# Sums over tokens as one full-array product per batch, gate values as four products with block-diagonal weights, both casts of a bank pair ahead of both subtractions, and four joint places

## The chip, the cores and the metric

The kernel runs on one core of one Trainium2 chip. The metric is the device time of one execution in microseconds, the median of the runs of a kernel. A core has a matrix engine (TensorE, PE in the rows; its weight loads stand apart as PEld), a vector engine (VectorE, DVE), a scalar engine (ScalarE, ACT), GpSimd (POOL) and a sync engine (SyncE, SP), which issues nearly all transfers here. TensorE can be used as one array of 128x128 or as several tiles; a row such as `64*32` gives the tile's rows and columns.

## The reference, cut to what matters

Eight batches, eight heads, 576 tokens, 64 channels a head, 32 memory slots; then a mixture of eight experts over 4608 tokens of 512 channels, hidden width 1024.

```python
a = np.exp(phi - np.max(phi, axis=2, keepdims=True))
a = a / (np.sum(a, axis=2, keepdims=True) + 1e-09)      # over tokens
k_m = np.einsum('bhsm,bhsd->bhmd', a, k)
v_m = np.einsum('bhsm,bhsd->bhmd', a, v)
scores = scale * np.matmul(q, k_m.transpose(0, 1, 3, 2))
attn = softmax(scores)
x = rows(np.matmul(attn, v_m))
...
logits = x @ w_gate + modality_bias[modality_id]
e_idx = np.argmax(logits, axis=1)
gate_w = softmax(logits)[np.arange(N), e_idx]
...
h = np.maximum(x[mask] @ w1[e], 0.0)
out[mask] = gate_w[mask, None] * (h @ w2[e])
```

## The kernel before, in words

**Tiling.** Batches go in pairs, two half-arrays of 64 rows (`NG` = 2 groups `g`) by four strips of 32 columns (`HG` = 4 heads a group). The memory products `kv_products` (L408) use TensorE as eight tiles of 64x32: 72 matmuls over nine chunks of tokens, written `64*32` in the rows. Each float32 matmul of this kind leaves two records in the trace, so 72 are x144 there. The sums of the exponentials over the tokens (`sums`, folded over the chunks by GpSimd long before) follow in the same tiles: eight matmuls of one column against `ones_c` (L416). They give the softmax's denominators `den`, `rec` on VectorE, with which ScalarE scales the products into `kvn`. `first_products` and `first_sums` are the forms for batch 0.

**Weights folded into values.** The expert's first weights are multiplied by the memory values once per batch: `value_products` (L776, 64*32, eight matmuls for each half of 512 hidden columns), then split into a high part `vwh` (a cast by ScalarE) and a low part `vwl` (the product less the cast, by VectorE). The attention weights `xa`, `xb` are split into high and low likewise (`xah`, `xal`, `xbh`, `xbl`). `hidden` (L831) and `outputs` (L868) then run three full-array products for each tile, high by high, low by high, high by low. These two lines are nearly all of the matrix work. `relu` gives `hh` (ScalarE, L844) and `hl` (VectorE, L848), `gated` gives `ob` (ScalarE, L881), which is stored by SP.

**Gate.** `mem_gate` (L546) multiplies the memory values by `w_gate` in eight matmuls 64*32 of eight columns, at the end of the scores (L571) of the same batch; `gate_values` (L554) copies the two groups' results from two banks to `vg` with two VectorE copies. `logits` (L713) reads `vg` later, as 128*32 tiles.

**Order.** Nothing is left to a scheduler. A planner, `weave`, merges a list of attention stages with a list of expert stages by estimated takes (`TAKES`) and due times, and the calls are issued in that order on every engine. The table `JOINT` says, for batch b, behind which output step (tile, f) the joint stands; tile `None` counts as 4, and a batch without an entry has (2 + b % 2, 7). A joint is: the kv products of batch b+2, the sums, the value products of batch b+1 for the first half of the columns (into two single banks of `pe`) and for the second half (`other_values`, into a pair of banks), and the two transposes (`turn`, L150) of `kvn`. The functions themselves call the casts and subtractions, so ScalarE and VectorE have these queued in the order of the calls. There are four single PSUM banks `pe`, used in turn, and two pairs.

**The split of a pair.** `value_split` goes bank by bank, cast then subtraction (`split`). In a pair both banks are one PSUM tile, and the program makes the second bank's cast on ScalarE wait for the first bank's subtraction on VectorE; for the single banks there is no such wait.

## Time and profile before

| | |
|---|---|
| median of 3 runs | 381.92 us (380.41 to 382.25) |
| profiled execution | 380.38 us, span 378.6 us |
| mean granted clock of TensorE | 0.998 |
| TensorE busy | 370.4 us, 98% of the span |
| VectorE, ScalarE, GpSimd busy | 66%, 37%, 12% |
| TensorE's share of the chain that ended last | 88% |

Of the profile one reads first who is busy, then the chain of waits, then the timeline of TensorE at the places that the change touches. The start times of successive matmuls tell what one costs; its busy time is longer, since matmuls overlap in the array, and the times on the rows of a group are of its first instruction.

### The profile page before, as it was taken

How to read it: one execution, taken by the hardware profiler on the slowest of the kernel's cores; microseconds unless marked ns; L12 is line 12 of the kernel's file. 1: busy time of each engine (PE TensorE's matmuls, PEld its weight loads, DVE VectorE, ACT ScalarE, POOL GpSimd, SP SyncE). 2: the span in 40 equal slices, each digit the busy share in tenths (PEclk: the TensorE clock that was granted, in tenths of full speed). 3: DMA queues.
4: the chain of work that ended last, by engine and by line, in shares of the span. 5: the costliest groups of instructions: out<-in, count | busy, mean ns of one | idle time of the engine just before them, and what ended most of it. 6: DMA issues, size and time to landing. Idle time of an engine off the chain costs nothing.

```text
span 378.6 us, 9983 instructions
## 1 busy us (share of the span) xinstructions
PE 370.4 (98%) x4045; PEld 308.5 (81%) x4045; DVE 248.6 (66%) x618; ACT 139.7 (37%) x328; POOL 46.1 (12%) x110
## 2 busy tenths in 40 slices
PE   6899999999999999999999999999999999999996
PEld 2677887889878898898987889797987979697986
DVE  4788758885958797868855689567874538750400
ACT  2382433524344054323415244431623306240401
POOL 3148030022130030004000030004000000000000
PEclk9999999999999999999999999999999999999999
DMA  8999668969969547583653737760232102321112
GB/s 290 348 377 239 110 121 250 292 114 304 282 113 287 216 72 141 155 311 61 110 167 99 270 70 128 214 205 2 56 110 74 29 2 55 119 64 30 30 35 56
DMA packets 93979, 56.89 MB, mean 150 GB/s; under 512 B 69732, under 2 KB 75108, under 8 KB 93924
## 3 DMA queue, kind: packets, MB, share of 16 engines
q1 hardware_dynamic: 93648, 55.87, 53.9%
q8 instruction: 33, 0.54, 0.6%
q10 hardware_dynamic: 276, 0.30, 0.2%
q14 instruction: 22, 0.18, 0.2%
HBM read 37.28 MB, written 18.87 MB: 148 GB/s over the span
## 4 chain that ended last, share of the span: by engine, by line
PE 88%; DVE 5%; DMA 3%; ACT 2%; issue 1%; SPq 1%; ACTq 0%; DVEq 0%
PE pe L868 48%; PE pe L831 26%; PE pair L408 4%; DMA raw<-in_moe_w_dram 2%; PE pe L776 2%; PE pair L571 2%; PE pe L912 2%; PE pair L776 1%; PE pair L713 1%; DMA ph<-in_phi_dram 1%; DVE vwl L156 1%; PE pair L150 1%; DVE top L310 1%; DVE a L650 0%; DVE sa L640 0%
## 5 line engine op out<-in xcount | busy, mean ns | idle before, releaser
L868 PE MATMUL pe<-w2h,hh 128*128 128x512 f32 x280 | 111.3, 397 | 0.0
L868 PE MATMUL pe<-w2h,hl 128*128 128x512 f32 x280 | 109.4, 391 | 0.0
L868 PE MATMUL pe<-w2l,hh 128*128 128x512 f32 x280 | 107.2, 391 | 0.0
L848 DVE SCALAR_TENSOR_TENSOR hl<-pe,hh 128x256 fp32r<-128x256 f32 (+2 forms) x158 | 56.7, 389 | 35.3 <-ACT hh L844 34.6
L844 ACT ACTIVATE hh<-pe 128x256 fp32r<-128x256 f32 (+2 forms) x158 | 52.5, 361 | 33.2 <-PE pe L831 32.6
L868 PEld LDWEIGHTS pe<-w2h,hh 128*128 128x128 f32 x280 | 52.6, 188 | 11.9 <-DVE vwl L156 0.8
L868 PEld LDWEIGHTS pe<-w2l,hh 128*128 128x128 f32 x280 | 52.5, 188 | 11.2
L868 PEld LDWEIGHTS pe<-w2h,hl 128*128 128x128 f32 x280 | 52.7, 188 | 9.8
L881 ACT ACTIVATE ob<-pe,gates 128x512 f32<-128x512 f32 x35 | 23.9, 688 | 68.6 <-PE pe L868 40.2
L831 PE MATMUL pe<-xbh,vwh 128*128 128x320 f32 x128 | 40.3, 314 | 0.1
L831 PE MATMUL pe<-xbh,vwl 128*128 128x320 f32 x128 | 39.6, 309 | 0.0
L831 PE MATMUL pe<-xbl,vwh 128*128 128x320 f32 x128 | 39.6, 309 | 0.0
L831 PE MATMUL pe<-xah,vwh 128*128 128x256 f32 x124 | 35.3, 287 | 0.4 <-DVE hl L848 0.4
L831 PE MATMUL pe<-xal,vwh 128*128 128x256 f32 x124 | 34.9, 283 | 0.0
L831 PE MATMUL pe<-xah,vwl 128*128 128x256 f32 x124 | 34.9, 283 | 0.0
L831 PEld LDWEIGHTS pe<-xah,vwh 128*128 128x128 f32 x124 | 23.6, 192 | 2.7 <-ACT vwl L793 0.8
L831 PEld LDWEIGHTS pe<-xbh,vwh 128*128 128x128 f32 x128 | 24.0, 188 | 1.4 <-issue 0.5
L344 POOL COPY ts<-tm 32x4 f32<-32x4 f32 x24 | 5.0, 210 | 165.2 <-DVE tm L336 164.4
L831 PEld LDWEIGHTS pe<-xbl,vwh 128*128 128x128 f32 x128 | 24.1, 188 | 0.3
L831 PEld LDWEIGHTS pe<-xbh,vwl 128*128 128x128 f32 x128 | 24.0, 188 | 0.0
L831 PEld LDWEIGHTS pe<-xal,vwh 128*128 128x128 f32 x124 | 23.7, 192 | 0.2
L831 PEld LDWEIGHTS pe<-xah,vwl 128*128 128x128 f32 x124 | 23.7, 192 | 0.0
(178 smaller groups left out, 465.5 us busy)
## 6 DMA issues: line engine op xcount, KB each, us to landing
out_dram<-ob SPq DMA_DIRECT2D x72, 128.0 KB, 2.4
q_sb<-in_q_dram SPq DMA_DIRECT2D x112, 72.0 KB, 3.1
kv_sb<-in_k_dram SPq DMA_DIRECT2D x6, 1152.0 KB, 6.4
kv_sb<-in_v_dram SPq DMA_DIRECT2D x6, 1152.0 KB, 9.2
ph<-in_phi_dram SPq DMA_DIRECT2D x13, 288.0 KB, 8.1
kv_sb<-in_k_dram SPq DMA_DIRECT2D x4, 576.0 KB, 5.6
kv_sb<-in_v_dram SPq DMA_DIRECT2D x4, 576.0 KB, 6.1
raw<-in_moe_w_dram SPq DMA_DIRECT2D x2, 1024.0 KB, 7.8
```

Of the source, the lines that this page charges most:

```text
L150: nc.tensor.transpose(dst, src, ident[:rows, :rows])
L156: nc.vector.tensor_tensor(l, src, h.bitcast(F32), op=ALU.subtract)
L344: nc.gpsimd.tensor_copy(ts_[BL * a:BL * (a + 1)], live["tm"][BL * o:BL * (o + 1)])
L408: nc.tensor.matmul(live["kvp"][M * j:M * (j + 1), g], lhsT=pe[half, j, c * M:(c + 1) * M], rhs=kv_sb[half, :, j, c * D:(c + 1) * D], start ...
L571: nc.tensor.matmul(sc[g][M * j:M * (j + 1), a, 0:QC * BL], lhsT=kvT[b][rows, 0, M * j:M * (j + 1)], rhs=qT[rows, j, a], start=True, stop=T ...
L776: nc.tensor.matmul(pvs[g][M * j:M * (j + 1), :], lhsT=vT[b][rows, j, :], rhs=raw1[rows, j, cols], start=True, stop=not more, tile_position ...
L831: nc.tensor.matmul(ph[:, 0:n], lhsT=(vl if k == 2 else vh)[:, g, cols], rhs=xl if k == 1 else xh, start=(g == k == 0), stop=(g == NG - 1 a ...
L844: nc.scalar.activation(hs[0][:, f, h0:h0 + p1 - p0], live["ph", f][:, p0:p1], AF.Relu)
L848: nc.vector.scalar_tensor_tensor(hl, live["ph", f][:, p0:p1], 0.0, hh.bitcast(F32), op0=ALU.max, op1=ALU.subtract)
L868: nc.tensor.matmul(po, lhsT=tile_columns(hl if n == 1 else hh, f, t), rhs=(w2l if n == 2 else w2h)[:, f, :], start=(f == n == 0), stop=(f ...
L881: nc.scalar.activation(ob, po, AF.Copy, scale=gate_of(b, t))
L912: nc.tensor.matmul(po, lhsT=x, rhs=w2s[w][:, f, cols], start=(f == i == 0), stop=(f == FCH - 1 and i == 2),)
```

## The change

It does five things. The eight sum products of a batch become one product of the whole array, `sums` of all heads as weights and an indicator `groups` (128x2, one for the rows of group g, else zero) as the moving side. The eight gate products become four of 128 rows by 32 columns with 16 moving columns, whose weights `wg` hold `w_gate` in two diagonal blocks and zeros elsewhere; so one copy to `vg` is enough instead of two. `wg` is set to zero by GpSimd and loaded by two DMAs on SP instead of one, between the two halves of the first expert weights (`raw`). `value_split` calls both casts, then both subtractions. And in `JOINT` the joint of b=2 goes from (2, 1) to (3, 1), that of b=3 from (3, 6) to (3, 4), that of b=5 from (3, 7) to (4, 6).

```diff
-    JOINT = {1: (4, 1), 2: (2, 1), 3: (3, 6)}
+    JOINT = {1: (4, 1), 2: (3, 1), 3: (3, 4), 5: (4, 6)}
...
+    groups = const.tile([P, NG], F32, name="groups")
...
-    wg = const.tile([P, KCH, E], F32, name="wg")
+    wg = const.tile([P, KCH, NG, E], F32, name="wg")
...
-        nc.sync.dma_start(wg, w_gate.rearrange("(a p) e -> p a e", p=P))
+        for g in range(NG):
+            rows = slice(D * g, D * (g + 1))
+            nc.sync.dma_start(wg[rows, :, g], w_gate.rearrange("(a p) e -> p a e", p=P)[rows])
...
-        for j in range(HG):
-            for g in range(NG):
-                half = slice(QP * g, QP * (g + 1))
-                nc.tensor.matmul(
-                    pk[M * j:M * (j + 1), g, 2 * D:2 * D + 1], lhsT=sums[half, j], rhs=ones_c[half],
-                    start=True, stop=True, tile_position=(QP * g, M * j),
-                )
+        nc.tensor.matmul(live["psum"], lhsT=sums.rearrange("p j m -> p (j m)"), rhs=groups, start=True, stop=True)
...
         for j in range(HG):
-            for g in range(NG):
-                rows = slice(D * g, D * (g + 1))
-                nc.tensor.matmul(
-                    to[g][M * j:M * (j + 1), 0, GATE:GATE + E], lhsT=vT[b][rows, j], rhs=wg[rows, j],
-                    start=True, stop=True, tile_position=(D * g, M * j),
-                )
+            nc.tensor.matmul(
+                to[0][M * j:M * (j + 1), 0, GATE:GATE + NG * E], lhsT=vT[b][:, j], rhs=wg[:, j].rearrange("p g e -> p (g e)"),
+                start=True, stop=True, tile_position=(0, M * j),
+            )
...
-        for g in range(NG):
-            nc.vector.tensor_copy(vg[b // 2][:, g, o:o + E], to[g][:, 0, GATE:GATE + E])
+        nc.vector.tensor_copy(
+            vg[b // 2][:, :, o:o + E], to[0][:, 0, GATE:GATE + NG * E].rearrange("p (g e) -> p g e", g=NG)
+        )
...
     def value_split(hf):
-        for g, pv in enumerate(live.pop(("pv", hf))):
-            split([x[:, g, hf * 512:(hf + 1) * 512] for x in vws], pv)
+        value_upper(hf)
+        value_lower(hf)
...
+        nc.gpsimd.memset(wg, 0.0)
```

In the order of TensorE, the joint of b=5 (kv products of batch 7, value products of batch 6) stood like this before; 24 output steps of tile `None` follow the transposes, and hidden products behind them.

```order
L408 MATMUL pair_3972<-kv_sb,exp 32x128 x72
L416 MATMUL pair_3972<-ones_c,sums 32x1 x8
L776 MATMUL pe<-raw_104,kvT_84 32x512 x8
L776 MATMUL pair_4074<-raw_104,kvT_84 32x512 x8
L150 MATMUL pair_4087<-ident,kvn 128x128 x2
L868 MATMUL pe<-w2h,hh 128x512
L868 MATMUL pe<-w2h,hl 128x512
L868 MATMUL pe<-w2l,hh 128x512
L868 MATMUL pe<-w2h,hh 128x512
```

Now, with the lines of the changed kernel (L411 for L408, L765 for L776, L151 for L150, L857 for L868, L820 for L831):

```order
L411 MATMUL pair_3925<-kv_sb,exp 32x128 x72
L416 MATMUL pair_3925<-groups,sums 128x2
L765 MATMUL pe<-raw_105,kvT_85 32x512 x8
L765 MATMUL pair_4020<-raw_105,kvT_85 32x512 x8
L151 MATMUL pair_4033<-ident,kvn 128x128 x2
L857 MATMUL pe<-w2h,hh 128x512
L857 MATMUL pe<-w2h,hl 128x512
L857 MATMUL pe<-w2l,hh 128x512
L820 MATMUL pe<-xah,vwh 128x256
L820 MATMUL pe<-xal,vwh 128x256
```

The sums are one instruction in another tiling, between products of eight tiles; and the joint moved behind 21 of the 24 output steps, so that three are left ahead of the hidden products of batch 6, which read the new `vwh` and `vwl`.

At the end of the scores of a batch, on TensorE, the gate values stood like this before.

```order
L571 MATMUL pair_2567<-q_sb_99,kvT_82 32x288
L546 MATMUL pair_2566<-wg,kvT_82 32x8
L546 MATMUL pair_2567<-wg,kvT_82 32x8
L546 MATMUL pair_2566<-wg,kvT_82 32x8
L546 MATMUL pair_2567<-wg,kvT_82 32x8
L546 MATMUL pair_2566<-wg,kvT_82 32x8
L546 MATMUL pair_2567<-wg,kvT_82 32x8
L546 MATMUL pair_2566<-wg,kvT_82 32x8
L546 MATMUL pair_2567<-wg,kvT_82 32x8
L868 MATMUL pe<-w2h,hh 128x512
```

Now:

```order
L560 MATMUL pair_2522<-q_sb_100,kvT_83 32x288
L560 MATMUL pair_2523<-q_sb_100,kvT_83 32x288
L534 MATMUL pair_2522<-wg,kvT_83 32x16 x4
L857 MATMUL pe<-w2h,hh 128x512
L857 MATMUL pe<-w2h,hl 128x512
```

Eight instructions in the tiling of the scores became four in a tiling that neither neighbour has.

On ScalarE, the joint of b=1 (value products of batch 2), before; in brackets is the engine whose semaphore an instruction waits for.

```order
L690 CAST xah<-aT 128x512
L155 CAST vwh<-pe 128x512 [waits PE_49] x2
L155 CAST vwh<-pair_1852 128x512 [waits PE_49]
L155 CAST vwh<-pair_1852 128x512 [waits DVE_49]
L528 COPY kvT_81<-pair_1865 128x256 [waits PE_49]
```

Now:

```order
L679 CAST xah<-aT 128x512
L774 CAST vwh<-pe 128x512 [waits PE_49] x2
L774 CAST vwh<-pair_1820 128x512 [waits PE_49]
L774 CAST vwh<-pair_1820 128x512
L518 COPY kvT_82<-pair_1833 128x256 [waits PE_49]
```

The rows stand in the same order; the second cast of the pair has lost its wait for VectorE.

## Rows read from the trace of the kernel before

**Rows 1.** The page's busy times of the engines (busy us, share of the span, instructions) and the shares of the chain that ended last.

```profile
PE 370.4 (98%) x4045; PEld 308.5 (81%) x4045; DVE 248.6 (66%) x618; ACT 139.7 (37%) x328; POOL 46.1 (12%) x110
...
PE 88%; DVE 5%; DMA 3%; ACT 2%; issue 1%; SPq 1%; ACTq 0%; DVEq 0%
```

**Rows 2.** The group of the sums among TensorE's instructions by line, whole span: busy us and mean ns of one, then idle time before them.

```profile
L416 PE MATMUL pair<-ones_c,sums 64*32 64x1 f32 x112 | 2.3, 169 | 0.0
```

**Rows 3.** TensorE in order of time, at a place where output products (128*128) give way to value products (64*32) and come back: start us, busy us, line, operation, names, shapes, count.

```profile
60.43 0.39 PE L868 MATMUL pe<-w2h,hl 128*128 128x512 f32 x1
60.65 0.39 PE L868 MATMUL pe<-w2l,hh 128*128 128x512 f32 x1
60.97 1.09 PE L776 MATMUL pe<-raw,kvT 64*32 64x512 f32 x16
```

**Rows 4.** The same view at the joint of b=2: the sums, the value products, the two transposes.

```profile
147.50 0.26 PE L416 MATMUL pair<-ones_c,sums 64*32 64x1 f32 x13
147.60 0.61 PE L776 MATMUL pe<-raw,kvT 64*32 64x512 f32 x1
...
149.63 0.44 PE L150 MATMUL pair<-ident,kvn 128*128 128x128 f32 x2
149.82 0.48 PE L868 MATMUL pe<-w2h,hh 128*128 128x512 f32 x1
```

**Rows 5.** The same view at the joint of b=1, from the first value product to the transposes.

```profile
110.93 0.59 PE L776 MATMUL pe<-raw,kvT 64*32 64x512 f32 x1
...
112.79 0.44 PE L150 MATMUL pair<-ident,kvn 128*128 128x128 f32 x2
```

**Rows 6.** The same view at the end of a batch's scores: the gate products and the output product behind them.

```profile
172.48 0.25 PE L546 MATMUL pair<-wg,kvT 64*32 64x8 f32 x16
172.66 0.50 PE L868 MATMUL pe<-w2h,hh 128*128 128x512 f32 x1
```

**Rows 7.** The chain of waits between 28 and 46 us (start us, us, what), and ahead of its last row TensorE's last product before 43 us from the timeline.

```profile
31.55 0.17 DVE vg L554
...
32.01 0.17 DVE vg L554
...
42.45 0.70 ACT ob L881
...
42.74 0.31 PE L831 MATMUL pe<-xbh,vwl 128*128 128x320 f32 x1
...
43.19 2.02 PE pe L831 x12
```

**Rows 8.** VectorE in order of time at the joint of b=1; in brackets the idle time before an instruction and what ended it.

```profile
116.39 0.63 DVE L156 TENSOR_TENSOR vwl<-pair,vwh 128x512 fp32r<-128x512 f32 x1
117.66 0.69 DVE L156 TENSOR_TENSOR vwl<-pair,vwh 128x512 fp32r<-128x512 f32 x1 [0.65 <-ACT vwh L155]
118.27 0.81 DVE L650 TENSOR_TENSOR a<-a,ra 128x640 f32<-128x640 f32 x1
...
119.95 0.38 DVE L848 SCALAR_TENSOR_TENSOR hl<-pe,hh 128x256 fp32r<-128x256 f32 x1
121.10 0.76 DVE L848 SCALAR_TENSOR_TENSOR hl<-pe,hh 128x256 fp32r<-128x256 f32 x2 [0.77 <-ACT hh L844]
```

**Rows 9.** ScalarE in the same stretch.

```profile
117.05 0.59 ACT L155 CAST vwh<-pair 128x512 fp32r<-128x512 f32 x1 [2.78 <-DVE vwl L156]
...
120.06 0.72 ACT L690 CAST xbh<-aT 128x640 fp32r<-128x640 f32 x1 [1.29 <-DVE aT L656]
120.69 1.20 ACT L844 ACTIVATE hh<-pe 128x256 fp32r<-128x256 f32 x4
```

**Rows 10.** TensorE in the same stretch, hidden products of batch 2.

```profile
119.82 0.28 PE L831 MATMUL pe<-xal,vwh 128*128 128x256 f32 x1
119.94 0.28 PE L831 MATMUL pe<-xah,vwl 128*128 128x256 f32 x1
120.39 0.39 PE L831 MATMUL pe<-xah,vwh 128*128 128x256 f32 x1 [0.17 <-DVE hl L848]
...
121.08 0.28 PE L831 MATMUL pe<-xah,vwl 128*128 128x256 f32 x1
121.58 0.39 PE L831 MATMUL pe<-xah,vwh 128*128 128x256 f32 x1 [0.22 <-DVE hl L848]
```

**Rows 11.** The view of waits, all engines, whole span: us in total, times, longest us.

```profile
ACT vwh L155 <- DVE vwl L156: 8.5, 5, 2.8
...
PEld pair L408 <- issue: 1.8, 5, 0.4
```

**Rows 12.** SP's issues around the load of `wg`, and the stretch from 8 to 12 us (busy us and count of PE, PEld, DVE, ACT, POOL, then granted clock, mean busy share of the DMA engines, GB/s).

```profile
10.58 0.61 SPq L253 DMA_DIRECT2D wg<-in_moe_w_gate_dram  x1
11.41 0.38 SPq L230 DMA_DIRECT2D raw<-in_moe_w_dram  x1
...
8.00:12.00 4.00, 3.48 (x92) 2.63 (x92) 3.34 (x9) 1.51 (x4) 0.00 (x0) 1.00 1.07 376
```

**Rows 13.** All engines in order of time at the joint of b=5: TensorE's transposes, VectorE's subtractions for the single banks and its last one for the pair.

```profile
289.08 0.44 PE L150 MATMUL pair<-ident,kvn 128*128 128x128 f32 x2
289.12 1.29 DVE L156 TENSOR_TENSOR vwl<-pe,vwh 128x512 fp32r<-128x512 f32 x2 [1.23 <-ACT vwh L155]
...
291.65 0.69 DVE L156 TENSOR_TENSOR vwl<-pair,vwh 128x512 fp32r<-128x512 f32 x1 [0.65 <-ACT vwh L155]
```

More of the change, by code (lines that the diff above doesn't have):

```diff
@@ L401, in kv_products @@
         pk = pair_of_banks(1)
-        live["psum"] = pk[:, :, 2 * D]
+        live["psum"] = pk[:, 0, 2 * D:2 * D + NG]
         live["kvp"] = pk[:, :, 0:2 * D].rearrange("p g (t d) -> p g t d", t=2)
@@ L427, in first_products @@
         if t == 0:
-            live["sums0"] = pk[:, :, 2 * D]
+            live["sums0"] = pk[:, 0, 2 * D:2 * D + NG]
         tiles = [(j, g, slice(QP * g, QP * (g + 1))) for j in range(0, HG, 2) for g in range(NG)]
@@ L440, in first_sums @@
         sums = live["pe", 0][1]
-        for g in range(NG):
-            for j in range(0, HG, 2):
-                half = slice(QP * g, QP * (g + 1))
-                nc.tensor.matmul(
-                    live["first", 0][g][M * j:M * (j + 2), 2 * D:2 * D + 1],
-                    lhsT=sums[half, j:j + 2].rearrange("p j m -> p (j m)"), rhs=ones_c[half],
-                    start=True, stop=True, tile_position=(QP * g, M * j),
-                )
+        nc.tensor.matmul(live["sums0"], lhsT=sums.rearrange("p j m -> p (j m)"), rhs=groups, start=True, stop=True)
     def first_divide():
@@ L543, in mem_gate @@
         for j in range(HG):
-            for g in range(NG):
-                rows = slice(D * g, D * (g + 1))
-                nc.tensor.matmul(
-                    to[g][M * j:M * (j + 1), 0, GATE:GATE + E], lhsT=vT[b][rows, j], rhs=wg[rows, j],
-                    start=True, stop=True, tile_position=(D * g, M * j),
-                )
+            nc.tensor.matmul(
+                to[0][M * j:M * (j + 1), 0, GATE:GATE + NG * E], lhsT=vT[b][:, j], rhs=wg[:, j].rearrange("p g e -> p (g e)"),
+                start=True, stop=True, tile_position=(0, M * j),
+            )
     def gate_values(b, to):
         o = E * (b % 2)
-        for g in range(NG):
-            nc.vector.tensor_copy(vg[b // 2][:, g, o:o + E], to[g][:, 0, GATE:GATE + E])
+        nc.vector.tensor_copy(
+            vg[b // 2][:, :, o:o + E], to[0][:, 0, GATE:GATE + NG * E].rearrange("p (g e) -> p g e", g=NG)
+        )
     def q_turn(b, c0, n, js):
@@ L1344, in attn_moe @@
         nc.gpsimd.memset(ones_c, 1.0)
+        for g in range(NG):
+            for r in range(NG):
+                nc.gpsimd.memset(groups[QP * r:QP * (r + 1), g:g + 1], float(g == r))
         ones_r = wk.tile([1, P], F32, name="ones_r")
```

## The prediction

> **What bounds the kernel now.** I read first who is busy and what the chain that ended last is made of: TensorE is busy 98% of the span and holds 88% of the chain, VectorE 66%, ScalarE 37% [rows 1]. So an edit off TensorE is worth something only where TensorE waits for it, and an edit on TensorE costs what it takes there, with nothing beside it to hide in. Second I read TensorE's timeline for starts that come later than the steady pitch. Behind the first 45 us there are few: the pitch of output products is 0.22 us [rows 3] nearly everywhere, and the largest late starts are two in the hidden products of batch 2 behind the joint of b=1 [rows 10]. In the first 45 us the chain leaves TensorE once, through VectorE and ScalarE, for the gate of batch 0 [rows 7]. Third I read, at the edited places, what one change of tiling takes, since both edits of matmuls trade instructions for changes of tiling. TensorE's clock was granted in full (1.00, the 2.4 GHz level) in the stretch of the start that I read [rows 12].
>
> **The price of a change of tiling.** Output products start 0.22 apart; the first product in another tiling starts 0.32 behind the last of them (60.65 to 60.97) [rows 3]. So a change costs 0.10 us beyond the work itself. Against that stands the price of a small instruction in tiles: the sums' records begin at 147.50 and the first value product at 147.60 [rows 4], so sixteen records, with mean busy times of 169 ns [rows 2], take 0.10 us together, because they overlap in the array. The Trainium skill, "TensorEngine Tiling (Array Packing)", section Instruction Overhead, says that each matmul has about 60 cycles of overhead and that one column takes as long as sixty; by that rule the fourteen records that go would be worth 14 x 25 ns = 0.35 us a batch, an estimate at 2.4 GHz. The trace disagrees for packed tiles: all sixteen take 0.10.
>
> **Sums.** From the first sum (147.50), right behind the last kv product's start, to the transposes (149.63) is 2.13 us now [rows 4]. Afterwards: the last kv product streams out and the array changes tiling, 0.20 (0.10 of the 128 columns, an estimate, and 0.10 of the change); the product of the whole array leaves two records, and two transposes, which also leave two, take 0.19 to the next start [rows 4] with 128 columns each, so with two columns I take 0.10; the change back is 0.10; then the value products from an empty start to the transposes, 110.93 to 112.79, 1.86 [rows 5]. That is 2.26, so +0.13 a joint. Bounds: if the change overlaps with the streaming of the neighbours, -0.1 (the records go and nothing comes); with the transposes' whole 0.19 and another 0.1 for the first weights, +0.35. There are five joints with value products behind the sums: +0.65. For two other batches the sums are followed by full-array products, so a change stands there now too, and only its place moves: +0.1 each for the second record, +0.2. For the first batch TensorE waits for the sums of exponentials anyway: 0, bounds 0 to 0.15. **Sums together +0.85** (-0.7 to +2.2).
>
> **Gate values.** Now the first gate record starts at 172.48 and the output product at 172.66 [rows 6]: 0.18, of which 0.10 is the change from 64*32 to 128*128 that any order needs. Afterwards there are two changes, 64*32 to 128*32 and on to 128*128. The second is paid already; the first is +0.10, the second record of the four new tiles, with nothing ahead of it in its tiling, is another 0.10 by the same 0.10 as for the sums, and the records that go give back 0.04 to 0.08. So +0.15 a batch, for seven batches (in batch 0 the neighbours are 32*32, and the gate has a change on either side already): **+1.05** (0 to +2.1).
>
> **One copy instead of two.** In batch 0 the chain runs through VectorE: the first copy at 31.55 (0.17), 0.30 of issue, the second at 32.01 (0.17), then everything up to the gates, `ob`, and TensorE at 43.19 [rows 7]. One copy less shortens that chain by 0.46. TensorE sits idle at its end only 0.30 (the product ahead starts at 42.74 and its 320 columns stream in 0.15, by the 0.12 of 256 columns [rows 10], so to 42.89), so the gain is **-0.30** (0 to -0.46). In later batches the copies lie beside output products: 0.
>
> **Both casts first.** ScalarE's cast of the pair's second bank waits for VectorE's first subtraction in five joints, 8.5 us in all, up to 2.78 [rows 9, 11]. With both casts first, VectorE's two subtractions run without the 0.65 between them [rows 8]. Who waits for that? Only behind the joint of b=1: VectorE goes on with `a`, `aT` and `hl` (118.27 to 119.95), ScalarE's `xbh` waits for `aT`, and `hh`, then `hl` at 121.10, follow it [rows 8, 9]; TensorE's hidden products start at 120.39 and 121.58 for banks that `hl` frees [rows 10], where the pitch of 0.12 makes them due at 120.06 and 121.20: 0.33 and 0.38 late, 0.71 together. Moving VectorE and ScalarE forward by 0.65 takes away nearly all: **-0.60** (0 to -0.71). The other four joints have output products behind them, whose operands are ready; they have no late start to give back: 0. The cover is the output steps behind each; where the joint moves it changes, below.
>
> **The joints' places.** Of b=2 and b=3 the joint moves among output steps (128*128 before and behind): same work, no late start before, several microseconds of output products behind: 0, bounds -0.3 to +0.3. Of b=5 it moves behind (4, 6), so that only three output products lie between the transposes and the hidden products of batch 6, where 24 lay. Counted from the start of the transposes: these take 0.2, the three products 0.8 with the late first start, so the hidden products begin at +1.0 with a pitch of 0.12. Their first tile reads the low part of single bank 0 in its third product (+1.2) and of bank 1 in its sixth (+1.6); the fifth tile, 24 products later, reads the pair's in its third (+4.1). VectorE's subtractions of the single banks run from 289.12 to 290.41, so they end at +0.7 and +1.3; the pair's last one ends at 292.34, +3.3, and at +2.6 without the 0.65 [rows 13]. So it fits by 0.3 to 1.5 us: 0, bounds 0 to +0.9, the last if the `ob` of tile None comes late on ScalarE behind the casts and holds a single bank that the hidden tiles want. Queued behind the subtractions on VectorE are `hl` of these tiles; the four transposes of queries there come ahead now, on data that landed long before.
>
> **Start.** GpSimd, busy 12% of the span [rows 1], gets five more memsets while TensorE warms up: 0. SP issues one DMA more ahead of the second half of `raw`: the one that exists takes 0.61 of SP, and 0.83 to the next issue [rows 12]. The DMA engines are saturated at that time (share 1.07, 376 GB/s) [rows 12], so a later issue goes behind a backlog: 0, bounds 0 to +0.8, since value products do wait for that data.
>
> **Sum.** +0.85 + 1.05 - 0.30 - 0.60 = +1.0 us. The profiled execution took 380.38 us (span 378.6, and 1.8 outside it); it would take 381.4. It is at the low end of the three runs, whose median is 381.92, so the median would be 382.9.
>
> **Rivals.**
> A, instructions go, changes are hidden. If the drains overlap with the neighbours' streams, the sums give 7 x -0.1, the gates 8 x -0.06, the copy -0.3, the casts -0.65, and the short idles of TensorE's sequencer ahead of the packed kv products (1.8 us in five places [rows 11]) shrink a little with fewer instructions, -0.3: 381.92 - 2.4 = 379.5. For it: TensorE's weight loads run beside it, 308 of 370 us [rows 1]. Against it: the 0.10 stands in the trace at each change of tiling that I looked at. The rule on overhead of the Trainium skill, "TensorEngine Tiling (Array Packing)", points to this side.
> B, the joint of b=5. Its cover falls from 24 products to three, and it decides from the point where the subtractions of the single banks end later than +1.2, or the freed `pe` bank of tile None later than the fourth tile: 0.9 us, and with the second half of `raw` late, which has the same sign, 0.6 more: 382.9 + 0.9 = 383.8 to 384.4. For it: ScalarE has five casts, the copy of `kvT` and `ob` within 3 us. Against it: the counted slack.
> C, no gain from the casts and the copy. The late starts move to the next link (ScalarE's `hh` behind `xbh`, `lg` behind the logits): 382.9 + 0.9 = 383.8.
>
> **How the numbers follow.** Forecast, with ends from the cost of changes alone (382.0 to 383.7): 0.50. A 0.22, B 0.16, C 0.12. A measurement of this kernel can tell about 0.5%, 1.9 us, from no change: below 380.0 is faster, above 383.8 slower. A's time lies below 380.0 in most of its cases, 0.18 of 0.22; of B and C some two thirds lie above, 0.19, and of the forecast another 0.06 with the changes of tiling at their upper bounds. Faster 0.18, same 0.57, slower 0.25. The range goes from A's time, 379.5, to 384.6, where B ends with the sums' terms 0.2 higher.
>
> **What would show it.** At each joint, the first sum to the transposes should take 2.2 to 2.4 us (2.13 now), and the product of the whole array stand alone between two gaps. From the first gate record to the output product should be about 0.33 in place of 0.18. ScalarE's wait for the subtraction should be gone from the view of waits, and the two late starts of the hidden products of batch 2 with it. Between the gate product of batch 0 and the hidden products that now start at 43.19, the chain should be 0.3 shorter. At the joint of b=5 the hidden products of batch 6 should run at 0.12. What would make the prediction wrong: changes of tiling that cost nothing or 0.2 each (twelve new pairs of them, 1 to 2 us either way), or a wait of TensorE behind one of the moved joints.

## The result, and the profile after

The changed kernel took 383.71 us (median of 18 runs, 381.99 to 385.67), the kernel before 380.63 us (18 runs, 380.01 to 382.25): ratio 1.0073, 95% interval 1.0061 to 1.0086. The forecast was 382.9, 1.0 above the median then known; the time lies in the range and on the forecast side, but the loss is 3.1 us, three times the sum, and with 0.7% beyond the 0.5% within which it had most of its chance. That the time comes within 0.8 us of the forecast is partly luck: the 381.92 that the forecast started from, a median of three runs, was 1.3 us above the median of the 18.

In the profiled execution (384.72 us, 1.0 above the median; span 382.9 against 378.6 before) TensorE is again what bounds. The useful measure is **TensorE's line**, from the start of the first kv product of batch 1 to the start of the last matmul, which leaves out the start of the kernel: 50.03 to 375.08 before, 325.05 us; 51.02 to 379.00 after, 327.98 us. So of the 4.3 us between the two spans 2.93 lie on the line, 0.99 ahead of it and 0.4 behind it. Each line is that of one execution; the two profiles of one kernel in experiment 8 have lines 0.3 apart. Below, a *burst* is the kv products, sums and value products of one batch, a *late start* is what a product starts later than the steady pitch of its kind, and a *stall* is a pause inside a burst that work of another engine does not explain. The page's busy times of the engines, after, against [rows 1]:

```profile
PE 373.6 (98%) x3877; PEld 307.8 (80%) x3877; DVE 248.3 (65%) x610; ACT 139.7 (36%) x328; POOL 46.7 (12%) x115
```

TensorE has 168 records fewer and is busy 3.2 us longer. The largest single piece stands where the forecast saw nothing, in the kv products of batch 1. TensorE in order of time, after (start us, busy us, line, names, shapes, count; in brackets the idle time ahead):

```profile
51.02 2.01 PE L411 MATMUL pair<-kv_sb,exp 64*32 64x128 f32 x127
54.49 0.51 PE L411 MATMUL pair<-kv_sb,exp 64*32 64x128 f32 x17 [1.45 <-issue]
54.93 0.38 PE L416 MATMUL pair<-groups,sums 128*128 128x2 f32 x2
55.17 0.48 PE L857 MATMUL pe<-w2h,hh 128*128 128x512 f32 x1
```

The 144 records stop behind the 127th, with 1.72 us from that start to the next; nothing that the profile shows ends the idle time. Before, the 144 took 2.02 us without a pause. The DMA view of the changed kernel from 52 to 53 us has one transfer of the kind that carries instructions (queue, kind: packets, MB, share):

```profile
q8 instruction: 1, 0.02, 5.5%
```

In the trace it starts 1.07 us behind the first kv product. This became the theory to test: TensorE had run out of instructions.

The joint, here that of b=2, against [rows 4], and the end of a batch's scores, against [rows 6], in the same view of the changed kernel:

```profile
155.98 0.38 PE L416 MATMUL pair<-groups,sums 128*128 128x2 f32 x2
156.30 1.09 PE L765 MATMUL pe<-raw,kvT 64*32 64x512 f32 x16
157.18 1.06 PE L765 MATMUL pair<-raw,kvT 64*32 64x512 f32 x16
158.18 0.44 PE L151 MATMUL pair<-ident,kvn 128*128 128x128 f32 x2
...
174.58 1.20 PE L560 MATMUL pair<-q_sb,kvT 64*32 64x288 f32 x32
175.71 0.26 PE L534 MATMUL pair<-wg,kvT 128*32 128x16 f32 x8
175.89 0.50 PE L857 MATMUL pe<-w2h,hh 128*128 128x512 f32 x1
```

One product of two columns holds TensorE for 0.32 us until the tiles start again. From the first kv product to the next output product a joint takes 4.56 us (4.59 once) in place of 4.31 to 4.34 (4.41 and 4.61 in two joints that had short pauses before), and where no value products follow 2.42 to 2.45 in place of 2.21 (by the places without a pause in these kernels and in experiments 1 and 8; the kernel before itself took 2.25 and 2.29, with short pauses). The scores with their gate take 1.32 (174.58 to 175.89) in place of 1.17 in four of seven places, and 1.24 us more in all seven together.

At the joint of b=1 VectorE and ScalarE, against [rows 8, 9], did what was hoped: two casts in one run, two subtractions in one run.

```profile
117.00 1.10 ACT L774 CAST vwh<-pair 128x512 fp32r<-128x512 f32 x2
...
119.72 1.22 DVE L787 TENSOR_TENSOR vwl<-pair,vwh 128x512 fp32r<-128x512 f32 x2
```

The 48 hidden products of batch 2, which had 0.89 us of late starts [rows 10], have none. At the joint of b=5 [rows 13] three output products are left, and the hidden products follow at their pitch, with ScalarE and VectorE just in time:

```profile
297.57 0.44 PE L151 MATMUL pair<-ident,kvn 128*128 128x128 f32 x2
...
298.55 0.28 PE L820 MATMUL pe<-xah,vwh 128*128 128x256 f32 x1
298.66 0.29 PE L820 MATMUL pe<-xal,vwh 128*128 128x256 f32 x1
298.78 0.28 PE L820 MATMUL pe<-xah,vwl 128*128 128x256 f32 x1
...
298.96 1.29 DVE L787 TENSOR_TENSOR vwl<-pair,vwh 128x512 fp32r<-128x512 f32 x2 [0.18 <-ACT vwh L774]
```

In the chain of waits of batch 0's gate, against [rows 7], one copy has gone, and yet `ob` comes as long behind the gate product as before (32.09 to 43.45, before 31.10 to 42.45):

```profile
32.48 0.17 DVE vg L541
32.66 0.29 issue
32.95 0.93 DVE a L613 x2
...
34.75 1.09 DVE a L619
```

The last row is the subtraction of the maxima behind the transposes. In the chain of the kernel before it stands as:

```profile
33.89 0.98 DVE a L630
```

And ahead of the line, in this execution, TensorE's granted clock fell to half, its 1.2 GHz level, for 3.4 us (stretch, then busy us of PE, PEld, DVE, ACT, POOL, granted clock, DMA share, GB/s); the kernel before had 1.00 in the same stretch:

```profile
9.90:12.80 2.90, 2.90 (x64) 2.85 (x56) 1.67 (x4) 0.46 (x2) 0.00 (x0) 0.50 1.06 357
```

That comes and goes between executions: the kernel before has mean granted clocks from 0.991 to 1.000 over its runs, the changed kernel from 0.994 to 1.000. Of the 14 profiled executions five show the half clock somewhere between 8.7 and 13.3 us, two of them with the sums and gate of the kernel before there (experiments 2 and 11). A sixth is counted with them by its pace: in experiment 1 the record of the clock begins at 14.4 us, and the first kv products of batch 0 take 4.12 us in place of 2.20. The line of these six begins at 50.3 to 52.1 us, that of the eight others at 49.4 to 50.5. It is why the line is compared below and not the totals alone.

### The profile page after: what moved, and what is told of

The parts are those of the page before. It is cut to its first block, busy times and chain, and to the rows that moved or that the text cites. A ratio compares the mean times of both kernels' runs of the same rounds, so it can differ in the third digit from the quotient of the medians.

```text
span 382.9 us, 9653 instructions
## 1 busy us (share of the span) xinstructions
PE 373.6 (98%) x3877; PEld 307.8 (80%) x3877; DVE 248.3 (65%) x610; ACT 139.7 (36%) x328; POOL 46.7 (12%) x115
## 4 chain that ended last, share of the span: by engine, by line
PE 91%; DVE 4%; DMA 1%; ACT 1%; issue 1%; ACTq 0%; POOL 0%; DVEq 0%; POOLq 0%
PE pe L857 48%; PE pe L820 26%; PE pair L411 4%; PE pe L765 2%; PE pair L560 2%; PE pe L901 2%; PE pair L702 1%; DMA row<-n_moe_modality_bias_dram 1%; PE pair L765 1%; PE pair L430 1%; PE pair L151 1%; PE pair L416 1%; PE pair L582 1%; PE pe L430 1%; DVE a L613 0%
## 5 line engine op out<-in xcount | busy, mean ns | idle before, releaser
L857 PE MATMUL pe<-w2h,hh 128*128 128x512 f32 x280 | 111.3, 398 | 0.0
L857 PE MATMUL pe<-w2h,hl 128*128 128x512 f32 x280 | 109.3, 390 | 0.0
L857 PE MATMUL pe<-w2l,hh 128*128 128x512 f32 x280 | 107.2, 391 | 0.0
L857 PEld LDWEIGHTS pe<-w2h,hh 128*128 128x128 f32 x280 | 52.6, 188 | 11.9 <-issue 0.8
L857 PEld LDWEIGHTS pe<-w2l,hh 128*128 128x128 f32 x280 | 52.5, 188 | 11.3
L857 PEld LDWEIGHTS pe<-w2h,hl 128*128 128x128 f32 x280 | 52.7, 188 | 9.8
L820 PE MATMUL pe<-xbh,vwh 128*128 128x320 f32 x128 | 40.2, 314 | 0.2 <-ACT ob L870 0.2
L820 PE MATMUL pe<-xbl,vwh 128*128 128x320 f32 x128 | 39.6, 309 | 0.0
L820 PE MATMUL pe<-xbh,vwl 128*128 128x320 f32 x128 | 39.6, 309 | 0.0
L820 PE MATMUL pe<-xah,vwh 128*128 128x256 f32 x124 | 35.2, 286 | 0.5 <-ACT xah L668 0.5
L820 PE MATMUL pe<-xal,vwh 128*128 128x256 f32 x124 | 34.9, 283 | 0.0
L820 PE MATMUL pe<-xah,vwl 128*128 128x256 f32 x124 | 34.9, 283 | 0.0
L820 PEld LDWEIGHTS pe<-xah,vwh 128*128 128x128 f32 x124 | 23.6, 191 | 2.7 <-ACT xah L668 1.6
L820 PEld LDWEIGHTS pe<-xbh,vwh 128*128 128x128 f32 x128 | 24.1, 188 | 1.1 <-ACT ob L870 0.5
L820 PEld LDWEIGHTS pe<-xbl,vwh 128*128 128x128 f32 x128 | 24.1, 188 | 0.3
L820 PEld LDWEIGHTS pe<-xbh,vwl 128*128 128x128 f32 x128 | 24.1, 188 | 0.0
L820 PEld LDWEIGHTS pe<-xal,vwh 128*128 128x128 f32 x124 | 23.7, 191 | 0.2
L820 PEld LDWEIGHTS pe<-xah,vwl 128*128 128x128 f32 x124 | 23.7, 191 | 0.0
```

The costliest lines, as they stand in the source:

```text
L820: nc.tensor.matmul(ph[:, 0:n], lhsT=(vl if k == 2 else vh)[:, g, cols], rhs=xl if k == 1 else xh, start=(g == k == 0), stop=(g == NG - 1 a ...
L857: nc.tensor.matmul(po, lhsT=tile_columns(hl if n == 1 else hh, f, t), rhs=(w2l if n == 2 else w2h)[:, f, :], start=(f == n == 0), stop=(f ...
```

## The experiments

Two theories at first. **A**: the stall is TensorE waiting for its own instructions; a packet of them came only inside the burst of kv products, which goes through instructions faster than any other part (144 records in 2 us, where output products make one in 0.22), and the change, which removes instructions, moved the bursts against the packets. **B**: sums, casts, joints or late data make it.

**1. Fourteen more warm-up matmuls in the changed kernel.**

```diff
-    BUSY = 64, 10
+    BUSY = 78, 10
```

> The changed kernel with 14 more tiny warm-up matmuls at the very start (78 instead of 64), where TensorE waits for VectorE anyway. 28 TensorE instructions more put the kv products of batch 1 at the place in the instruction stream where they stood before the change. Theory A (TensorE ran out of instructions at 52.8 us: it fetches them in packets of 16 KB, the packet came only inside the dense burst of kv products, and the change moved the burst against the packets): the 1.7 us stall inside the kv products of batch 1 is gone, and the time falls from 383.7 to about 382.0, unless another burst runs dry instead. Theory B (the stall comes from the sums, the casts, the joints or from data that came late): the stall stays and the time stays at 383.7.

383.36 us (6 runs; ratio to before 1.0065, 1.0040 to 1.0090). The stall is gone:

```profile
52.12 2.27 PE L411 MATMUL pair<-kv_sb,exp 64*32 64x128 f32 x144
54.32 0.38 PE L416 MATMUL pair<-groups,sums 128*128 128x2 f32 x2
```

No burst of batches 1 to 7 has a stall, and the line is 326.84, 1.14 shorter than the change's, although 0.63 came in near its end (one output product starts 0.85 behind the last, at 369.3). The time did not fall to 382.0, and the profiled execution, 1.4 above the median, ran at half pace ahead of 14.4 us. So A is borne out on the place, and missed on the total.

**2. Fourteen fewer in the kernel before.**

```diff
-    BUSY = 64, 10
+    BUSY = 50, 10
```

> The kernel before with 14 fewer tiny warm-up matmuls (50 instead of 64), nothing else. Theory A: the kv products of batch 1 come to stand where the changed kernel has them, a stall of about 1.7 us appears there, and the time goes from 380.6 to about 382.3; the two idles of 0.3 us in the kv products of batches 3 and 7 move. Theory B: nothing moves, 380.6.

385.76 us (6 runs; ratio 1.0134, 1.0101 to 1.0166): five microseconds slower by fourteen tiny matmuls left out ahead of everything, where 382.3 was expected. The stall appears in the kv products of batch 1, at the same instruction, and larger ones in the sums of batches 3 and 7; behind that of batch 3 the clock is at half for 3.4 us besides. TensorE in order of time:

```profile
50.34 2.01 PE L408 MATMUL pair<-kv_sb,exp 64*32 64x128 f32 x127
53.27 0.51 PE L408 MATMUL pair<-kv_sb,exp 64*32 64x128 f32 x17 [0.92 <-issue]
...
114.19 0.19 PE L416 MATMUL pair<-ones_c,sums 64*32 64x1 f32 x1 [2.05 <-issue]
114.19 0.88 PE L776 MATMUL pe<-raw,kvT 64*32 64x512 f32 x7
```

B fell with this: sums, casts, joints and data are those of the kernel before.

**3. The old split in the changed kernel.**

```diff
-        value_upper(hf)
-        value_lower(hf)
+        for g, pv in enumerate(live.pop(("pv", hf))):
+            split([x[:, g, hf * 512:(hf + 1) * 512] for x in vws], pv)
```

> The changed kernel with the split of a value pair as before: cast, subtraction, cast, subtraction. No TensorE instruction is added or taken away, so by theory A the stall in the kv products of batch 1 stays as it is. If both casts first gave the 0.9 us that the hidden products of batch 2 became shorter by, that comes back: 383.7 to about 384.6, with late starts in the hidden products of batch 2 again. The rival, that those late starts went because the joint's surroundings moved, gives 383.7. At the joint of b=5, where only three output products are left ahead of the hidden products, the old split could cost 0.3 us more.

385.78 us (6 runs; ratio 1.0131, 1.0100 to 1.0162). The line is 328.62. The stall is there again behind the 127th record (1.12 us). Late starts: 0.70 in the hidden products of batch 2, 0.26 behind the joint of b=2 and 0.32 behind that of b=5, where the changed kernel has none. The first of these, TensorE in order of time:

```profile
123.37 0.28 PE L820 MATMUL pe<-xah,vwl 128*128 128x256 f32 x1
123.86 0.39 PE L820 MATMUL pe<-xah,vwh 128*128 128x256 f32 x1 [0.22 <-DVE hl L837]
```

So both casts first are worth 1.28 on the line of the changed kernel, 0.58 of it as cover for joints that moved. The median is 2.1 above the changed kernel's, more than the lines tell (0.64 longer with a stall that is 0.6 shorter); the runs spread from 383.25 to 387.18, and what the others lost was not profiled.

**4. The old sums in the changed kernel** (the 16 records of L416 and the four small products of batch 0 again, the rest as changed).

> The changed kernel with the sums over tokens as before, eight small matmuls in the tiling of the kv products (four for the first batch). If the changes of tiling cost what was forecast, +0.85 together, that comes back: 0.13 to 0.2 at each of five joints and 0.1 to 0.2 at the two other places. By theory A the 12 instructions more ahead of the kv products of batch 1 move the stall there too: 383.7 less 0.9, and less 0 to 1.7 more, so 381.1 to 382.8. Rival, the sums cost nothing and the stall is not of instructions: 383.7.

385.11 us (6 runs; ratio 1.0119, 1.0097 to 1.0141), slower than with the new sums, where 381.1 to 382.8 was expected. The four places without a stall take 2.21 and 4.31 to 4.34 again, so the lasting cost is gone; but three bursts stall in their value products, 2.3, 2.0 and 1.0 us. One joint at its old length, and one of those that stall:

```profile
153.11 2.25 PE L411 MATMUL pair<-kv_sb,exp 64*32 64x128 f32 x144
...
157.42 0.48 PE L870 MATMUL pe<-w2h,hh 128*128 128x512 f32 x1
...
242.35 1.11 PE L778 MATMUL pe<-raw,kvT 64*32 64x512 f32 x10
244.44 0.62 PE L778 MATMUL pe<-raw,kvT 64*32 64x512 f32 x3 [0.97 <-issue]
```

**5. The old gate in the changed kernel** (eight products, two copies, one load, no zeroed blocks).

> The changed kernel with the gate values as before (eight products in the tiling of the scores, two copies, one load, no zeroed blocks). Theory A in its present form: the lasting cost of the gate's changes of tiling is 0.14 to 0.2 us in each of seven batches, so from the kv products of batch 1 to the last product TensorE's line is 1.1 us shorter than in the changed kernel, apart from stalls in which TensorE waits for instructions; those (1.7 us in the changed kernel, in the kv products of batch 1) go or come with the 16 instructions more, each between 0 and 2.3 us. If the gate costs nothing, only stalls differ.

383.57 us (5 runs; ratio 1.0067, 1.0047 to 1.0088). The scores with the gate take 1.17 again, and late starts of 0.2 each come back in the hidden products of batches 4 and 6, as before the change. The gate of the batch that [rows 6] shows:

```profile
172.73 1.20 PE L559 MATMUL pair<-q_sb,kvT 64*32 64x288 f32 x32
173.72 0.25 PE L534 MATMUL pair<-wg,kvT 64*32 64x8 f32 x16
173.90 0.50 PE L856 MATMUL pe<-w2h,hh 128*128 128x512 f32 x1
```

Stalls: none in batch 1, 0.6 in batch 3, 1.5 in batch 5. The line is 327.47; without the stalls of either it is 0.9 shorter than the changed kernel's, or 1.2 without the late starts, where 1.1 was expected.

**6. The old joints in the changed kernel.**

```diff
-    JOINT = {1: (4, 1), 2: (3, 1), 3: (3, 4), 5: (4, 6)}
+    JOINT = {1: (4, 1), 2: (2, 1), 3: (3, 6)}
```

> The changed kernel with the joints' places as before, nothing else. Up to the joint of b=2 no instruction of TensorE moves, so by theory A the stall in the kv products of batch 1 must be there again, 1.1 to 1.7 us; behind it the bursts of batches 4, 5 and 7 stand elsewhere against the packets, so stalls of 0 to 2.3 us may appear there. The places themselves cost nothing: the hidden products behind the joint of b=5 have no late start in either. If the places mattered (the rival), hidden products behind the joints of b=2, 3 or 5 would start late in one of the two kernels.

386.31 us (4 runs; ratio 1.0152, 1.0130 to 1.0174). The stall of batch 1 stands at the same record:

```profile
49.82 2.01 PE L411 MATMUL pair<-kv_sb,exp 64*32 64x128 f32 x127
53.32 0.51 PE L411 MATMUL pair<-kv_sb,exp 64*32 64x128 f32 x17 [1.49 <-issue]
```

Stalls of 0.3 and 1.1 come in batches 4 and 7, and the clock was granted at half from 54.9 to 58.3. Hidden products start late behind no joint, in either kernel: with both casts first the places cost nothing, and gain nothing but another draw of stalls.

**7. Sums and gate as before: the casts and the joints' places alone.**

> The changed kernel with both the sums and the gate values as before, so only the casts and the joints' places remain of the change. Without stalls for instructions it should be 0.9 us faster than the kernel before on TensorE's line behind the joint of b=1, and have no lasting cost; its instructions stand where those of the kernel before stand up to the joint of b=2, so no stall in batch 1 and 0.3 in batch 3, and unknown ones (0 to 2.3) behind. Without new stalls 379.6, with them up to 382.

380.48 us (10 runs; ratio 1.0011, 0.9994 to 1.0028). All bursts at their old length but batch 4's, which stalls 1.9 us in the value products. Without that the line is 323.9.

**8. The casts alone, in the kernel before, and once more with more runs.**

> The kernel before with both casts of a pair ahead of both subtractions, nothing else: no TensorE instruction is added, removed or moved, unless waits are counted. If the two late starts in the hidden products of batch 2 come from the cast's wait, they go and the time falls by 0.9 us from 380.5 to 379.6; stalls for instructions stay where they are in the kernel before (0.3 in batches 3 and 7). If the gain needs the moved joints, 380.5.

379.46 us (10 runs; ratio 0.9983, 0.9965 to 1.0002).

> The kernel before with both casts of a pair first, once more, with more rounds, to see whether it beats the kernel before clear of noise. TensorE's line was 1.2 us shorter in its profile (0.8 from the late starts behind the joint of b=1, 0.4 from stalls for instructions that went). Expected 379.4, ratio 0.997 with an interval below 1. If the 0.4 was chance of one execution, ratio 0.998.

379.82 us (11 runs; ratio 0.9992, 0.9980 to 1.0004). The line is 323.86 and 324.15, 1.2 and 0.9 below the kernel before; the late starts in the hidden products of batch 2 fall from 0.89 to 0.15 and 0.18, and no burst stalls. It has the lowest medians of the study, yet neither interval is clear of 1, which the second expectation had asked for.

**9. The new sums ahead of the kv products, in the five joints** (`FROM` is 3, the batch of the first joint's kv products).

```diff
+        if b >= FROM:
+            nc.tensor.matmul(live["psum"], lhsT=sums.rearrange("p j m -> p (j m)"), rhs=groups, start=True, stop=True)
         for c in range(QC):
...
-        nc.tensor.matmul(live["psum"], lhsT=sums.rearrange("p j m -> p (j m)"), rhs=groups, start=True, stop=True)
+        if b < FROM:
+            nc.tensor.matmul(live["psum"], lhsT=sums.rearrange("p j m -> p (j m)"), rhs=groups, start=True, stop=True)
```

> The changed kernel with the new product for the sums issued ahead of the kv products in the five joints, where it stands beside output products in the same tiling; the first three batches as in the change. If the cost of the new sums is the pair of changes of tiling between tiled products and not the product, each joint takes 4.33 us or less from the first kv product to the next full-array one apart from the product itself (4.56 in the change, 4.31 before), so 1.2 us of TensorE's line in all; the product adds about 0.1 ahead. If the product itself costs it, 4.56 stays. No instruction is added, so by theory A the stall of 1.1 to 1.7 us in batch 1 stays.

384.10 us (4 runs; ratio 1.0091, 1.0062 to 1.0120). From the first kv product each joint takes 4.09, and the product ahead 0.1: 4.2 in place of 4.56. At one joint:

```profile
154.74 0.28 PE L408 MATMUL pair<-groups,sums 128*128 128x2 f32 x2
154.95 2.25 PE L413 MATMUL pair<-kv_sb,exp 64*32 64x128 f32 x144
...
159.04 0.48 PE L860 MATMUL pe<-w2h,hh 128*128 128x512 f32 x1
```

So the price is the changes of tiling, not the product. But in batch 3 TensorE now waits for GpSimd:

```profile
113.05 0.38 PE L408 MATMUL pair<-groups,sums 128*128 128x2 f32 x2 [0.95 <-POOL sums L305]
```

The line, 328.96, is no shorter. The stall of batch 1 (1.76 us from start to start) is there, and 1.6 us behind it the clock falls to half for 3.4 us; in the stretch of the stall it was still 1.00:

```profile
51.50:53.30 1.80, 0.31 (x23) 0.04 (x5) 0.58 (x1) 0.00 (x0) 0.22 (x1) 1.00 0.62 94
54.90:58.30 3.40, 3.40 (x11) 2.64 (x10) 0.32 (x1) 1.00 (x3) 0.00 (x0) 0.50 0.96 320
```

**10. The same with the casts alone and the old gate.**

> The kernel before with both casts first, and in the five joints the sums as one full-array product ahead of the kv products; gate values, places and the other sums as before. Each joint should take 4.2 to 4.3 us (4.31 with the small sums between), at most 0.1 saved each, so TensorE's line is 0 to 0.5 us shorter than with the casts alone, 323.4 to 323.9 us from the first kv product of batch 1, if no stall for instructions comes in; 28 fewer instructions a joint move the later bursts, so one of 0 to 2.3 us may, and then it is no faster.

382.99 us (7 runs; ratio 1.0078, 1.0043 to 1.0112): missed. Three joints take 4.09 and batch 6's 0.5 more, but batch 3's product comes 1.1 late behind GpSimd's sums, TensorE then stalls 2.6 in the kv products, and the clock is at half from 114.4 to 117.8. The line is 329.20.

**11. Two more full-array products between the tiles**, in batches 1 to 7 of the kernel with the casts alone, to price a change of tiling; they are additional work.

```diff
+        nc.tensor.matmul(
+            pk[:, 0, 3 * D:3 * D + NG], lhsT=sums.rearrange("p j m -> p (j m)"), rhs=groups, start=True, stop=True,
+        )
         for j in range(HG):
...
+        nc.tensor.matmul(
+            pk[:, 1, 3 * D:3 * D + NG], lhsT=sums.rearrange("p j m -> p (j m)"), rhs=groups, start=True, stop=True,
+        )
```

> The kernel before with both casts first, and in each batch from 1 to 7 two additional full-array products of two columns, one between the kv products and the small sums and one behind these; their results aren't used. It prices the change of tiling: the new sums made a joint 0.25 us longer by one product with one pair of changes, in place of sixteen records worth 0.10. So one more product between tiles costs 0.35, and two in a joint 0.7: 5.0 us from the first kv product to the next full-array one where it was 4.31. In batches 1 and 2, where full-array products follow anyway, 0.35 for the first and 0.1 for the second: 2.65 instead of 2.21. If a change costs nothing, 4.5 and 2.3. Stalls for instructions can come on top.

384.99 us (4 runs; ratio 1.0129, 1.0111 to 1.0148), with no stall. TensorE in order of time at one joint:

```profile
149.39 0.38 PE L414 MATMUL pair<-groups,sums 128*128 128x2 f32 x2
149.71 0.27 PE L420 MATMUL pair<-ones_c,sums 64*32 64x1 f32 x16
149.90 0.38 PE L424 MATMUL pair<-groups,sums 128*128 128x2 f32 x2
150.22 1.09 PE L783 MATMUL pe<-raw,kvT 64*32 64x512 f32 x16
```

The joints take 5.07, 0.75 more, and the two other places 2.93, 0.72 more. In a joint one such product with its changes costs 0.37, as expected; the two other places were expected at 2.65 and cost the same as a joint, though tiles stand on one side only of the second product.

## Why the prediction was right or wrong

**The total: in the range, in part by luck.** The forecast sum was +1.0, the line became 2.93 longer. Changes of tiling were dearer than forecast by 1.0, the copy gave 0.3 less, late starts gave 0.6 more, and 1.3 came from a cause that no term and no rival held. The time lies where the forecast ends with the dearest changes of tiling (383.7), and close to rivals B and C; it got there by another way.

**The balance on TensorE's line**, +2.93: sums 5 x 0.24 + 2 x 0.22 = +1.64; gates +1.24 (seven places, 0.14 to 0.26 each); late starts behind the joint of b=1 -0.89 and in batches 4 and 6 -0.35; stalls for instructions +1.8 where the kernel before has about 0.5 in its bursts, so +1.3. That makes 2.94. Two other lines follow from the same entries, with their own stalls and late starts put in: the old sums, 327.98 - 1.64 - 1.8 + 5.3 = 329.8, measured 329.90; the casts alone, without the stalls and with 0.74 less of late starts, 325.05 - 0.5 - 0.74 = 323.8, measured 323.86 and 324.15.

**Sums: right in mechanism, mis-sized.** Forecast +0.85, measured +1.64, inside the bounds. The kv products drain for 0.19, as forecast (0.20); the product and the change back were put at 0.20 and take 0.32 (155.98 to 156.30). The 0.10 taken for the product alone, out of the 0.19 of two transposes, was too low: with the 0.10 of the change back, 0.22 is left for it, near the whole 0.19 that was kept as the upper end.

**Gate: right.** +1.05 forecast, +1.24 measured. Only its place was wrong: from the gate's first record to the output product is 0.18 as before, and the extra stands ahead of it, behind the scores. Of the 1.24, 0.1 goes with a joint's place and not with the gate: the scores of batch 5 take 1.27 with the old gate and the new places (experiment 5), 1.17 before.

**One copy: wrong.** -0.30 was taken off the chain of batch 0, and it gave nothing. The step that failed is "one copy less shortens that chain by 0.46". Two rows show why: before, the transposes start 0.08 behind the second copy; after, they start 0.47 behind the only one, with the same 0.29 of issue between. What the chain waited for is mostly that pause after the first copy, and the second copy took its place behind it without much cost. The transposes do start 0.13 sooner behind the gate product (0.87 us in place of 1.00), but the subtraction of the maxima takes 0.1 us longer (the row of 1.09 against that of 0.98) and gives that back; both are so in all six profiles with the new gate against all eight with the old. The subtraction runs beside a product of GpSimd in either kernel; whether that holds it is not shown. A gain that was put at 0 came instead: the late starts of 0.2 each in the hidden products of batches 4 and 6 stand in all eight profiles with the old gate and in none of the six with the new. Whether the copy or the product does that was not tried apart.

**Both casts first: right.** Forecast -0.60; -0.70 to -0.74 by experiments 3 and 8, and the whole 0.89 goes together with the rest of the change.

**The joints' places: right, with a condition.** Nothing starts late behind the moved joints, as forecast, but only with both casts first: with the old split the joints of b=2 and b=5 cost 0.26 and 0.32. Rival B did not come; rival C did for the copy and not for the casts.

**What no step and no rival held: the supply of instructions.** Rival A took the row on idle time of the weight loads ahead of the kv products [rows 11] for idles that shrink with fewer instructions. Four of its five, 0.35 to 0.37 each, stand where output products give way to kv products, and stay in kernels without any stall (experiments 1 and 8); the fifth, 0.33 ahead of the last kv products of batch 7, is TensorE waiting for instructions, and fewer instructions move such waits rather than shrink them. That it is this, and not data or another engine, rests on the following. With the kv products of batch 1 at one place in the instruction stream the pause comes behind the 127th record in five kernels that differ in split, joints, sums' place and gate (the change and experiments 2, 3, 6 and 9); with 12 or more instructions more ahead of it, there is none (experiments 1, 4, 5). Adding fourteen unrelated matmuls removes it and removing fourteen makes it. In each of these five stalls a packet of queue 8 starts 0.07 to 1.13 us behind the first kv product, and resuming takes 2.4 to 2.8 us from there; in the nine profiles without this stall none starts inside this burst, and the last one ahead starts 3.1 to 4.4 us before it.

The plainest sign is in the numbering. Counted in TensorE's matmul records from the start, each stall that shows as idle time in any of the 14 profiles stands, to within two records, behind number 729, 1487, 1866, 1994, 2373, 2882, 3261 or 3390, whether the kernel has kv products, sums or value products there. From the first of these the others lie 6, 9, 10, 13, 17, 20 and 21 times about 126.5 records away, as the ends of equal packets would; the waits for GpSimd in experiments 9 and 10 (1284, 1342) do not. One pause outside the bursts, near the end in experiment 1, does not fit either. In bytes the packets are equal, 16 KB each. That queue 8 carries TensorE's instructions is an inference from these times: fourteen warm-up matmuls more or fewer, and nothing else, move its packet from 52.09 to 47.84 us and from 45.98 to 50.79. What decides when a packet is asked for, and why the same pause was 1.1 us in one kernel and 1.8 in another, stays open.

The Trainium skill, "Trainium Architecture — The Big Picture", section The software stack, says that the instruction streams are brought to each engine when the program is loaded. The trace does not bear that out for all of them: packets of instructions move throughout the execution, 32 of them on queue 8 in the changed kernel, from 11.29 to 369.83 us.

**The start** was forecast at 0 and is not settled: the 0.99 ahead of the line came together with the half clock. In the eight profiled executions without it the line begins at 49.4 to 50.0 us with the old single load (five) and at 49.8 to 50.5 with the new two (three), so some 0.3 us for the later data can't be excluded, inside the bounds given, nor shown from so few.

## What to carry to other kernels

Where instructions are short and dense, a change of their number is two edits: the one that was meant, and a new draw of where the engine runs out of instructions, here stalls of up to 2.6 us at up to three of seven places. Measure both by comparing stretches of the trace, and try a neutral pad ahead of everything before believing a total. A small product in a tiling of its own is dear between products of another (0.37 us here, and 0.24 net in place of sixteen small records that took 0.10), and cheap beside products of its own tiling, if its operands are ready by then. When two instructions wait on each other's engine in turn, both of one engine first is worth trying, and it gives joints room to move.

## What the runs showed of the hardware that was not expected

TensorE's instructions arrive while it runs, and a burst of 288 records in 2 us can outrun them: idle times of 0.3 to 2.6 us in kv products, sums or value products. After four of these stalls the granted clock was at half for 3.4 us: from 54.9 behind stalls that ended at 53.3 (experiments 6 and 9), from 114.4 and 114.5 behind stalls that ended at 113.7 and 114.2 (10 and 2); not after that of the changed kernel, which ended at 54.5, nor after those of 2.3, 2.0 and 1.9 us in experiments 4 and 7. Between 14.4 us and the last microseconds no profile has the half clock anywhere else. So a stall can cost more than its length; what tells the four from the others is not shown.
